# A new order of the attention steps in a fused local and pooled attention with a top-1 mixture of experts

## The chip, the cores and the metric

The kernel runs on one core of a Trainium2 chip. The metric is the device time of one execution in microseconds (us). Five engines work side by side: PE (matmuls; its weight loads are shown apart as PEld), DVE, ACT and POOL (elementwise work), and SP, which here mostly issues transfers. Each runs its own instructions strictly in program order, and they wait for each other through semaphores.

## The reference

Inputs are q, k and v of 8 batches, 8 heads, 576 positions and 64 features, and the weights of a router and of 16 experts.

```python
q_d, k_d, v_d = (x.reshape(B, H, 144, 4, D).mean(axis=3) for x in (q, k, v))
out_up = np.repeat(sm_attn(q_d, k_d, v_d), 4, axis=2)        # attention among means of four
mask = np.abs(pos[:, None] - pos[None, :]) < 4               # local attention, 7 keys wide
out_local = softmax(where(mask, q @ k.T / 8, -1e9)) @ v
x = (out_up + out_local).transpose(0, 2, 1, 3).reshape(4608, 512)
# each token: best of 4 groups, then best of its 4 experts, both by softmax
y = relu(x @ w1[g, e]) @ w2[g, e]                            # 512 -> 1024 -> 512
out = g_w * e_w * y
```

## The kernel before

The attention is cut into 16 units (two batches and two heads each). A unit is a chain of steps, each a method: the transfers `load_k`, `load_q`, `load_v` and `load_windows`; the sums over four positions `pool_q`, `pool_k`, `pool_v`; the local scores `s_local` (72 small matmuls for each head), their shift by the maximum `s_local_out`, `s_local_exp`, `soft_local_sum`, `soft_local`, and the transposes `turn_e`; the pooled scores `s_down`, `s_down_max`, `s_down_exp`, the transposes `turn_pd`, the product `out_down`, its transposes `turn_down`, and `down_store` and `load_down`, which take its result through DRAM into the lower rows of the window tile `vw`; the product `x_bank` of both attentions with `vw`; `store_x`, which writes the tokens to DRAM; `turn_x` and `logits`, the router's scores. A step that copies out of PSUM ends in `_out` and has a letter for its engine (A, D or P: ACT, DVE, POOL). Units 14 and 15 have only one buffer of `x` and of some other tiles (`of`), since the others are given up for the experts' weights (`change`).

After each fourth unit the router works on a quarter of the tokens: `scores_turn`, `choose`, `choose_first` (writes the one-hot tile `oh`), `places` (PE sums of `oh`), `places_out`, `lists_places` (tile `bo`), `lists` (tile `m`, two halves), `lists_add` (PE, tile `tab`). From `tab` come the token lists: `early_list`, `ranks`, `rank_lists`. After three quarters the expert with most room is known (`pick_early`); its first 256 tokens are gathered and computed while attention ends: `turn_in`, eight `hidden` (12 matmuls each) and eight `project` (6 matmuls each), with `weights_in` (transfers) and `weights_split` (each weight split into two parts, on ACT and then POOL or DVE). `begin` and `main` then run the 16 experts, PE almost without a pause.

What sets the order: the text `ORDER` at the end of the file, 966 steps, each with its engine letter where it has a choice. It is read from first to last with automatic scheduling turned off (`tc.manual_schedule()`), so each engine's program is the steps' instructions in the text's order.

```python
for line in ORDER.split("\n"):
    for step in line.split(";"):
        if step.strip():
            name, *args = step.split()
            do(name, [int(a) if a.isdigit() else a for a in args])
```

Of the kernel before, what the change touches and what calls it, by code (L numbers as in the profile page):

```python
# [19 lines left out]
P = 128  # L20
B, H, S, D = 8, 8, 576, 64
# [32 lines left out]
class Attention:  # L54
# [1146 lines left out]
soft_local_sum 0 D; turn_pd 0 2; s_local_out 1 0; load_k 3; turn_pd 0 1; turn_pd_out 0 1 A; turn_pd_out 0 0 A; soft_local 0
turn_pd_out 0 2 A; s_down 1; s_local_exp 1 0; pool_v 0; out_down 0; s_local_exp 1 1; turn_e 0 0; s_down_max 1; clear vs 1
turn_e 0 2; s_down_exp 1 0; soft_down 0 P; s_down_exp 1 1; load_windows 0; turn_e 0 1; soft_local_sum 1 D; turn_e_out 0 2 A
out_down_out 0 D; s_local 2 1; pool_k 2 P; s_local_out 2 1; load_q 3; constants; load_k 4; s_local 2 0; s_down_exp 1 2
turn_e_out 0 0 A; turn_down 0; turn_pd 1 0; turn_pd_out 1 0 A; turn_pd 1 1; load_v 1; s_local_out 2 0; pool_q 3 P; turn_down_out 0
# [4 lines left out]
turn_down 1; turn_pd_out 2 1 A; soft_local_sum 2 D; load_down 0 S; turn_pd_out 2 2 D; pool_v 3; load_v 4; out_down 2  # L1210
turn_down_out 1; s_local_out 3 1; x_bank 0 1; out_down_out 2 A; soft_down 2 D; load_k 5; turn_down 2; x_bank 0 2; x_bank_out 0 1 A
s_down 3; soft_local 2; clear_windows 2; down_store 1 S; pool_q 4 D; turn_down_out 2; x_bank_out 0 2 D; x_bank 0 0; turn_e 2 1
x_bank_out 0 0 A; s_down_max 3; s_down_exp 3 0; turn_x 0 1; turn_e 2 0; load_windows 1; s_down_exp 3 1; turn_x 0 0; turn_x_out 0 1 A
turn_e_out 2 1 D; turn_x_out 0 0 A; s_down_exp 3 2; down_store 2 S; load_down 1 S; turn_e 2 2; turn_e_out 2 0 A; load_k 6
pool_k 4 P; s_local 4 0; s_local_exp 3 1; pool_k 5 D; turn_e_out 2 2 D; store_x 0 A; s_local 4 1; turn_pd 3 0; turn_x 0 2
turn_pd 3 2; turn_pd_out 3 2 A; turn_x_out 0 2 A; s_local_out 4 1; x_bank 1 0; turn_pd_out 3 0 D; s_local_out 4 0; s_local_exp 3 0
x_bank 1 2; x_bank 1 1; load_weights; load_v 5; s_down 4; soft_local_sum 3 P; s_local_exp 4 0; soft_local 3; x_bank_out 1 2 A
turn_pd 3 1; logits 0; x_bank_out 1 0 A; s_down_max 4; s_local_exp 4 1; x_bank_out 1 1 A; turn_pd_out 3 1 A; turn_e 3 0
s_down_exp 4 2; turn_x 1 2; turn_e 3 1; pool_q 5 P; out_down 3; load_windows 2; turn_e_out 3 0 D; soft_local_sum 4 D; load_down 2 S
turn_x 1 0; s_down_exp 4 0; turn_e_out 3 1 A; soft_down 3 P; turn_x_out 1 2 A; s_local 5 0; out_down_out 3 A; load_k 7; load_q 6  # L1220
s_down_exp 4 1; load_v 6; turn_x 1 1; turn_e 3 2; s_local 5 1; turn_e_out 3 2 A; turn_pd 4 0; turn_x_out 1 1 A; turn_x_out 1 0 D
turn_pd_out 4 0 A; turn_down 3; soft_local 4; pool_v 4; s_local_out 5 0; x_bank 2 2; s_local_out 5 1; x_bank_out 2 2 A
turn_down_out 3; logits 1; turn_pd 4 1; load_q 7; x_bank 2 1; s_down 5; s_local_exp 5 1; soft_down 4 P; turn_pd_out 4 1 A
turn_pd 4 2; x_bank 2 0; turn_x 2 2; s_down_max 5; s_down_exp 5 0; s_down_exp 5 1; turn_pd_out 4 2 A; s_down_exp 5 2
x_bank_out 2 1 D; pool_q 6 D; turn_e 4 2; s_local 6 1; turn_x_out 2 2 D; x_bank_out 2 0 D; turn_e_out 4 2 A; pool_k 6 D; s_local 6 0
down_store 3 S; turn_pd 5 2; turn_e 4 0; turn_e 4 1; pool_v 5; turn_e_out 4 0 A; out_down 4; turn_pd_out 5 2 D; s_local_out 6 0
s_local_out 6 1; turn_x 2 0; load_q 8; out_down_out 4 A; load_windows 3; turn_e_out 4 1 D; turn_x_out 2 0 A; turn_down 4
s_local_exp 5 0; load_down 3 S; turn_down_out 4; load_windows 4; s_down 6; s_local_exp 6 0; turn_pd 5 1; turn_x 2 1; s_down_max 6
turn_pd 5 0; turn_pd_out 5 1 A; x_bank 3 0; soft_local_sum 5 D; turn_x_out 2 1 A; x_bank 3 1; turn_pd_out 5 0 A; s_down_exp 6 1
out_down 5; s_down_exp 6 0; down_store 4 S; soft_local 5; out_down_out 5 D; s_local_exp 6 1; turn_e 5 1; x_bank_out 3 0 A; pool_v 6  # L1230
soft_local_sum 6 D; s_local 7 0; soft_down 5 P; s_down_exp 6 2; pool_q 7 P; turn_e_out 5 1 A; x_bank_out 3 1 A; logits 2; load_q 9
x_bank 3 2; turn_x 3 0; turn_down 5; pool_q 8 P; x_bank_out 3 2 A; load_k 8; turn_e 5 0; turn_e 5 2; turn_x_out 3 0 A; pool_k 7 P
turn_down_out 5; turn_x 3 2; load_k 9; s_local_out 7 0; turn_pd 6 1; turn_e_out 5 0 A; pool_k 8 D; turn_e_out 5 2 A; turn_x 3 1
turn_x_out 3 2 A; s_local 7 1; load_down 4 S; turn_x_out 3 1 A; turn_pd_out 6 1 D; turn_pd 6 0; logits 3; store_x 1 A; turn_pd 6 2
load_v 7; turn_pd_out 6 0 A; s_local_out 7 1; s_local_exp 7 1; soft_local 6; turn_pd_out 6 2 D; x_bank 4 0; down_store 5 S
x_bank 4 2; x_bank_out 4 2 D; scores_out 0; load_windows 5; s_down 7; x_bank 4 1; scores_turn 0; x_bank_out 4 1 A; x_bank_out 4 0 D
scores_turn_out 0; out_down 6; turn_e 6 2; store_x 2 A; out_down_out 6 A; turn_e 6 0; s_down_max 7; turn_down 6; soft_down 6 P
pool_v 7; turn_e 6 1; s_down_exp 7 0; s_down_exp 7 2; choose 0; turn_down_out 6; s_local 8 0; s_down_exp 7 1; choose_exp 0
turn_e_out 6 2 D; s_local 8 1; turn_pd 7 0; s_local_out 8 0; turn_e_out 6 0 A; s_local_exp 7 0; turn_x 4 1; turn_e_out 6 1 A
turn_x 4 0; turn_pd 7 2; load_down 5 S; turn_x_out 4 1 A; turn_pd_out 7 0 A; s_local_out 8 1; soft_local_sum 7 D; turn_pd 7 1  # L1240
turn_x 4 2; turn_pd_out 7 1 D; store_x 3 A; turn_x_out 4 2 A; load_q 10; turn_x_out 4 0 A; s_down 8; turn_pd_out 7 2 A; x_bank 5 0
load_v 8; load_k 10; s_local_exp 8 0; choose_first 0; x_bank 5 1; x_bank 5 2; x_bank_out 5 0 A; s_local_exp 8 1; places 0
# [166 lines left out]
```

## Time and profile before

| | |
|---|---|
| runs of the kernel before | 766.26, 775.36, 776.48 us (median 775.36) |
| the profiled execution's own time | 768.92 us |
| its span (first to last instruction) | 767.2 us |
| busy share of the span: PE, DVE, ACT, POOL | 92%, 61%, 47%, 35% |
| mean granted TensorE clock | 0.953 of full |

Times in rows are in us from the span's start; a row of a timeline gives the start, the busy time, the engine, the line, the operation, the tiles written and read and the number of instructions, and in brackets the idle time before it with what ended it ("issue" is a wait for which the profile shows no other engine or transfer). A granted clock of 0.50 is 1.2 GHz and 1.00 is 2.4 GHz.

### The profile page before, as it was taken

To read this page: it belongs to the slowest core of one execution; us is meant where nothing else is said; L and a number is where in the kernel's file an instruction comes from. 1 tells how busy PE (TensorE), PEld (TensorE's weight loads), DVE (VectorE), ACT (ScalarE), POOL (GpSimd) and SP (SyncE) were. 2 spreads that over 40 slices of the span, in tenths; PEclk is the share of its full clock that TensorE was granted. 3 is DMA by queue.
4 is the path that set the end of the run, shared out by engine and by line. 5 is a ranking of instruction groups with operands and counts; after the bars stand their busy time and mean duration, and the time that the engine had idled before them with its cause. 6 is when DMAs were issued, how large, how long until landed. Compare 5 with 4: busy or idle time off the path is not lost. (4 is left out here: it accounts for less than half of the span.)

```text
span 767.2 us, 20003 instructions
## 1 busy us (share of the span) xinstructions
PE 703.1 (92%) x8116; PEld 636.8 (83%) x8117; DVE 464.3 (61%) x840; ACT 359.9 (47%) x791; POOL 268.1 (35%) x313
## 2 busy tenths in 40 slices
PE   6787988898887879999999999999999999999991
PEld 3665766677665769999999999999999999999891
DVE  7776858698885585664545454465465565556510
ACT  1535534575564525553434444445454455556410
POOL 8956547476652652103111221312302312320211
PEclk7879988999999999999999999999999999999997
DMA  8879899989898625855455555555646656665300
GB/s 261 229 201 239 236 247 266 236 232 259 211 207 249 170 88 193 273 171 191 134 177 178 159 176 175 184 184 175 220 149 203 225 165 212 210 213 178 131 26 23
DMA packets 167459, 146.83 MB, mean 191 GB/s; under 512 B 69908, under 2 KB 139540, under 8 KB 167364
## 3 DMA queue, kind: packets, MB, share of 16 engines
q1 hardware_dynamic: 142756, 115.02, 51.4%
q0 software_dynamic: 7088, 21.66, 8.2%
q10 hardware_dynamic: 17520, 8.85, 4.4%
q8 instruction: 64, 1.05, 0.6%
q14 instruction: 31, 0.25, 0.1%
HBM read 124.19 MB, written 22.29 MB: 191 GB/s over the span
## 5 line engine op out<-in xcount | busy, mean ns | idle before, releaser
L866 PE MATMUL ph<-xh,w1h 128*128 128x256 f32 (+13 forms) x512 | 162.3, 318 | 0.0
L837 POOL DMA_INDIRECT xg<-xd,gi x47 | 49.1, 1046 | 320.1 <-ACT yo L940 286.4
L866 PE MATMUL ph<-xl,w1h 128*128 128x256 f32 (+13 forms) x512 | 157.1, 309 | 0.0
L866 PE MATMUL ph<-xh,w1l 128*128 128x256 f32 (+13 forms) x512 | 157.1, 309 | 0.0
L825 DVE TENSOR_TENSOR w2l<-raww,w2h 128x1024 fp32r<-128x1024 f32 x61 | 74.5, 1223 | 72.9 <-ACT w2h L824 70.9
L914 PE MATMUL y<-hl,w2h 128*128 128x416 f32 (+11 forms) x384 | 115.3, 311 | 0.0
L914 PE MATMUL y<-hh,w2l 128*128 128x416 f32 (+11 forms) x384 | 114.3, 308 | 0.0
L824 ACT ACTIVATE w2h<-raww 128x1024 fp32r<-128x1024 f32 x64 | 67.6, 1057 | 73.4 <-PE y L914 61.6
L866 PEld LDWEIGHTS ph<-xh,w1h 128*128 128x128 f32 x512 | 97.4, 191 | 1.5 <-issue 0.2
L866 PEld LDWEIGHTS ph<-xl,w1h 128*128 128x128 f32 x512 | 97.5, 191 | 0.9
L866 PEld LDWEIGHTS ph<-xh,w1l 128*128 128x128 f32 x512 | 97.3, 190 | 0.3
L825 DVE TENSOR_TENSOR w1l<-raww,w1h 128x1024 fp32r<-128x1024 f32 x60 | 73.3, 1223 | 38.8 <-ACT w1h L824 33.8
L871 DVE SCALAR_TENSOR_TENSOR hl<-ph,hh 128x256 fp32r<-128x256 f32 (+13 forms) x128 | 60.3, 475 | 57.3 <-ACT hh L870 57.0
L870 ACT ACTIVATE hh<-ph 128x256 fp32r<-128x256 f32 (+13 forms) x128 | 53.7, 421 | 78.0 <-PE ph L866 75.3
L914 PE MATMUL y<-hh,w2h 128*128 128x416 f32 (+11 forms) x384 | 87.7, 312 | 0.0
L824 ACT ACTIVATE w1h<-raww 128x1024 fp32r<-128x1024 f32 x64 | 67.5, 1056 | 31.8 <-PE ph L866 27.1
L914 PEld LDWEIGHTS y<-hh,w2l 128*128 128x128 f32 x384 | 72.3, 188 | 0.1
L914 PEld LDWEIGHTS y<-hl,w2h 128*128 128x128 f32 x384 | 72.2, 188 | 0.1
L941 POOL DMA_INDIRECT out_dram<-yo,oi x47 | 48.1, 1023 | 67.8 <-ACT yo L940 36.0
L914 PEld LDWEIGHTS y<-hh,w2h 128*128 128x128 f32 x384 | 62.9, 188 | 0.1
L254 PEld LDWEIGHTS b_s<-kt,qT 64*32 64x32 f32 x2304 | 26.9, 116 | 29.2 <-issue 20.0
L427 PE MATMUL b_x<-vw,pt 128*32 128x128 f32 x1152 | 43.6, 298 | 7.5 <-DMA vw<-odd 3.5
(222 smaller groups left out, 1277.0 us busy)
## 6 DMA issues: line engine op xcount, KB each, us to landing
raww<-in_moe_w_dram SPq DMA_DIRECT2D x128, 512.0 KB
vw<-in_v_dram SPq DMA_DIRECT2D x62, 216.0 KB
kt<-in_k_dram SPq DMA_DIRECT2D x16, 576.0 KB
qT<-in_q_dram SPq DMA_DIRECT2D x16, 576.0 KB
xd<-x ACTq DMA_DIRECT2D x15, 576.0 KB
vs<-in_v_dram SPq DMA_DIRECT2D x32, 224.0 KB
vw<-odd SPq DMA_DIRECT2D x16, 144.0 KB
vs<-in_v_dram SPq DMA_DIRECT2D x32, 64.0 KB
```

Of the source, the lines that this page charges most:

```text
L254: nc.tensor.matmul(pt[32 * j : 32 * j + 32, g], s["qT"][r, b, 32 * blk : 32 * blk + 32], self.kt[u % 3][r, b, 32 * blk : 32 * blk + W], st ...
L427: self.nc.tensor.matmul(pt[32 * j : 32 * j + 32, t], self.of("pt", u)[:, 32 * lin : 32 * lin + 32], self.windows(u)[:, lin], start=True, s ...
L824: self.nc.scalar.activation(hi, raw, AF.Copy)
L825: eng.tensor_tensor(out=lo, in0=raw, in1=hi.bitcast(F32), op=ALU.subtract)
L837: self.nc.gpsimd.indirect_dma_start(out=xg[:w], out_offset=None, in_=self.xd[0:rows], in_offset=bass.IndirectOffsetOnAxis(ap=st["gi"][:w, ...
L866: nc.tensor.matmul(ph, a[:, k, cs], st[b][:, k], start=(n == 0), stop=(n == 11))
L870: nc.scalar.activation(hh, ph, AF.Relu)
L871: nc.vector.scalar_tensor_tensor(out=hl, in0=ph, scalar=0.0, in1=hh.bitcast(F32), op0=ALU.max, op1=ALU.subtract)
L914: nc.tensor.matmul(y, a[:, f % 2, cs], b, start=(f == 0 and n == 0), stop=(f == 7 and n == 2))
L941: i = nc.gpsimd.indirect_dma_start(out=self.out, out_offset=bass.IndirectOffsetOnAxis(ap=oi, axis=0), in_=yo[:m], in_offset=None, bounds_c ...
```

## The change

Only `ORDER` is replaced, by another order of the same 966 steps. `load_v` and `load_windows` now make a unit's entry where it is missing (`self.unit(u)` in place of `self.st[u]`), since `load_v 0` may come ahead of other steps of its unit; this adds no instruction. Every buffer, count, shape and function is as before, except for the letters:

| step | before | now |
|---|---|---|
| `pool_k` | 7 on DVE, 9 on POOL | 4 on DVE, 12 on POOL |
| `pool_q` | 7 on DVE, 9 on POOL | 6 on DVE, 10 on POOL |
| `turn_pd_out` | 8 on DVE, 40 on ACT | 14 on DVE, 34 on ACT |
| `turn_e_out` | 13 on DVE, 35 on ACT | 10 on DVE, 38 on ACT |
| `turn_x_out` | 8 on DVE, 40 on ACT | 11 on DVE, 37 on ACT |
| second half of `lists 3`; last `weights_split` | POOL; DVE | DVE; POOL |

Two pieces of the table, the first steps and those of the last quarter's router:

```diff
-shared_rows; clear kt 0; clear kt 1; warm_up 12; masks; masks_out D; load_k 1; clear E 1; s_local 0 1; clear_windows 0; pool_q 0 D
+masks; clear kt 0; clear E 0; masks_out D; load_k 1; warm_up 12; clear vs 0; shared_rows; pool_q 0 D; pool_k 0 D; load_v 0
...
-hidden 2; project 1; places 3; places_out 3; project 2; weights_split 2 w1 P; lists_places 3; lists 3 P; count 3
-weights_split 2 w2 P; hidden 3; lists_add 3; early_list 0; hidden 4; gather_late; project 3; ranks; weights_split 3 w1 P; hidden 5
+choose_first 3; weight 3; weights_split 1 w2 P; project 0; hidden 2; places 3; places_out 3; weights_in 3; lists_places 3
+weights_split 2 w1 P; project 1; hidden 3; lists 3 D; weights_split 2 w2 P; count 3; project 2; hidden 4; lists_add 3; early_list 0
```

**The start.** DVE before: the copies of `shared` into two tiles `pt`, the casts of the mask, then the pooled sums of unit 0 (`qd`, `kd`) and the shift of its local scores.

```order
L162 COPY pt_118<-shared 32x1152
L162 COPY pt_119<-shared 32x1152
L162 CAST idb<-idf 128x128
L162 CAST mask<-edge 128x342
L162 CAST mask<-edge 32x38 x4
L219 TENSOR_REDUCE qd_280<-qT_95 128x288
L234 TENSOR_REDUCE kd_282<-kt_91 128x288
```

DVE now:

```order
L162 CAST idb<-idf 128x128
L162 CAST mask<-edge 128x342
L162 CAST mask<-edge 32x38 x4
L162 COPY pt_118<-shared 32x1152
L162 COPY pt_119<-shared 32x1152
L219 TENSOR_REDUCE qd_240<-qT_95 128x288
L234 TENSOR_REDUCE kd_242<-kt_91 128x288
```

POOL before, at the same place (`edge` is what the mask is cast from, `vw_98` the first window tile):

```order
L123 MEMSET edge 128x38
L127 AFFINE_SELECT edge<-edge 32x38 x8
L129 AFFINE_SELECT edge<-edge 128x38 x2
L112 MEMSET E_130 128x9x10 x2
L140 MEMSET vw_98 128x4608
```

POOL now:

```order
L127 AFFINE_SELECT edge<-edge 32x38 x8
L129 AFFINE_SELECT edge<-edge 128x38 x2
L117 MEMSET kt_91 128x2x3 x2
L112 MEMSET E_129 128x9x10 x2
L114 MEMSET vs_109 48x512
L152 MEMSET shared 32x32
L154 AFFINE_SELECT shared<-shared 32x32 x2
L117 MEMSET kt_92 128x2x3 x2
L112 MEMSET E_130 128x9x10 x2
L140 MEMSET vw_98 128x4608
```

On DVE the two copies moved behind the casts, and on POOL the making of `shared` and the clears of `E_129` and `vs_109` moved ahead of the large clear of `vw_98`.

**The second quarter's choice.** DVE before, around `oh` (L583), on which PE's `places 1` waits; L285 to L287 are `soft_local_sum 11`, L323 to L325 `s_down_max 12`.

```order
L285 TENSOR_REDUCE sl_2924<-E_130 128x18
L286 TENSOR_SCALAR sl_2924<-sl_2924 128x18
L287 RECIPROCAL sl_2924<-sl_2924 128x18
L323 TENSOR_REDUCE mg_112<-b_d_12_3243 128x2
L323 TENSOR_REDUCE mg_112<-b_d_12_3244 128x2
L324 TENSOR_REDUCE mg_112<-b_d_12_3245 128x1
L325 TENSOR_SCALAR mg_112<-mg_112 128x5
L580 TENSOR_REDUCE m2x<-t 128x45
L581 TENSOR_TENSOR o<-t,m2x 128x180
L583 TENSOR_TENSOR oh<-o 128x144
```

DVE now:

```order
L291 TENSOR_TENSOR E_130<-E_130,sl_2923 128x9x76
L162 COPY xT<-b_xt_8_3212 128x3x128
L580 TENSOR_REDUCE m2x<-t 128x45
L581 TENSOR_TENSOR o<-t,m2x 128x180
L583 TENSOR_TENSOR oh<-o 128x144
L323 TENSOR_REDUCE mg_112<-b_d_12_3257 128x2
L323 TENSOR_REDUCE mg_112<-b_d_12_3258 128x2
L324 TENSOR_REDUCE mg_112<-b_d_12_3259 128x1
L325 TENSOR_SCALAR mg_112<-mg_112 128x5
```

`oh` is now written ahead of `s_down_max 12`, and `soft_local_sum 11` stands further up.

**The last quarter's lists.** DVE before, from `bo` to the table's readers (`hl` is the second part of a `hidden`'s result, so each `hl` row stands for one `hidden` on PE):

```order
L662 TENSOR_TENSOR bo<-b,place 128x1152
L657 TENSOR_TENSOR m_4748<-oh,chl 128x9x64
L623 COPY base<-pos_4709 128x16
L871 SCALAR_TENSOR_TENSOR hl<-ph,hh 128x256
L740 COPY th<-tab_4773 128x64
```

DVE now:

```order
L662 TENSOR_TENSOR bo<-b,place 128x1152
L871 SCALAR_TENSOR_TENSOR hl<-ph,hh 128x256
L657 TENSOR_TENSOR m_4767<-oh,chl 128x9x64 x2
L623 COPY base<-pos_4707 128x16
L871 SCALAR_TENSOR_TENSOR hl<-ph,hh 128x256
L740 COPY th<-tab_4798 128x64
```

Both halves of `m` are DVE's now, and two `hidden` instead of one stand between `places 3` and the table.

## Rows read from the trace of the kernel before

**Rows 1.** The page, its first two parts: busy us with share of the span and instructions, and the granted clock and DMA share in 40 slices of the span, in tenths.

```profile
PE 703.1 (92%) x8116; PEld 636.8 (83%) x8117; DVE 464.3 (61%) x840; ACT 359.9 (47%) x791; POOL 268.1 (35%) x313
...
PEclk7879988999999999999999999999999999999997
DMA  8879899989898625855455555555646656665300
```

**Rows 2.** Stretches of the span with each engine's busy time, the granted clock, the DMA share and GB/s: the attention's steady part, its end, the first expert's work beside the last router steps, and the experts.

```profile
20.00:230.00 210.00, 179.03 (x4319) 138.88 (x4307) 162.84 (x375) 110.96 (x373) 132.41 (x168) 0.90 0.91 233
230.00:256.00 26.00, 19.31 (x264) 14.58 (x261) 14.00 (x38) 12.01 (x27) 8.78 (x5) 0.92 0.85 227
256.00:289.00 33.00, 28.54 (x189) 24.80 (x188) 24.09 (x63) 10.39 (x22) 18.36 (x10) 0.91 0.43 127
289.00:767.00 478.00, 462.71 (x3168) 451.30 (x3166) 247.59 (x346) 223.12 (x362) 90.67 (x89) 0.99 0.53 173
```

**Rows 3.** Three of the rows of what PE waited for from 0 to 320 us: total us, times, the longest.

```profile
PE b_s L254 <- issue: 15.4, 8, 3.7
PE b_x L427 <- DMA vw<-odd: 3.5, 1, 3.5
PE tab L670 <- DVE m L657: 2.8, 2, 2.6
```

**Rows 4.** PE's timeline, waits put down to "issue" that are longer than 1 us: the first, the longest and the last of nine.

```profile
31.82 0.70 PE L254 MATMUL b_s<-kt,qT 64*32 64x38 f32 x56 [2.29 <-issue]
...
102.25 0.72 PE L254 MATMUL b_s<-kt,qT 64*32 64x38 f32 x29 [3.69 <-issue]
...
210.61 0.85 PE L254 MATMUL b_s<-kt,qT 64*32 64x38 f32 x44 [1.25 <-issue]
```

**Rows 5.** The stretch between the fifth and the sixth of these waits: busy time of PE, PEld, DVE, ACT and POOL with their instructions in brackets, clock, DMA share, GB/s.

```profile
102.25:124.02 21.77, 21.04 (x506) 16.48 (x507) 15.91 (x40) 10.60 (x38) 12.14 (x15) 0.86 1.06 264
```

**Rows 6.** The page's DMA queues, the one that carries instructions: packets, MB, share of 16 engines.

```profile
q8 instruction: 64, 1.05, 0.6%
```

**Rows 7.** The start: DVE's instructions of line 162 in one stretch (busy us and count, clock, DMA), then timeline rows of DVE, POOL and PE.

```profile
6.12:10.38 4.26, 4.24 (x1) 0.89 0.98 358
...
2.19 1.60 DVE L162 COPY pt<-shared 32x1152 f32<-32x1152 f32 x2 [0.98 <-POOL shared L154]
5.52 5.49 DVE L162 CAST mask<-edge 128x342 bf16<-128x342 f32 x5 [1.49 <-POOL edge L127]
6.09 3.94 POOL L140 MEMSET vw<- 128x4608 f32 x1
11.06 0.44 PE L249 MATMUL b_s<-mask,idb 128*128 128x342 bf16 x1 [4.71 <-DVE mask L162]
12.31 1.34 DVE L234 TENSOR_REDUCE kd<-kt 128x288 f32<-128x1152 f32 x1
13.57 0.51 DVE L268 TENSOR_REDUCE ml<-b_s 128x9 f32<-128x342 f32 x1
14.58 3.93 POOL L140 MEMSET vw<- 128x4608 f32 x1
17.22 1.34 DVE L219 TENSOR_REDUCE qd<-qT 128x288 f32<-128x1152 f32 x1
```

**Rows 8.** The second quarter's `places`: PE's wait for `oh`, DVE's work ahead of `choose_first` (busy us, count, clock, DMA), and the granted clock behind the wait.

```profile
181.61 0.22 PE L596 MATMUL pos<-oh,tri 128*128 128x144 bf16 x1 [1.73 <-DVE oh L583]
...
175.85:179.32 3.47, 3.37 (x9) 1.00 1.09 222
...
183.60:186.90 3.30, 3.30 (x83) 0.50 0.98 269
```

**Rows 9.** The end of the attention: SP's issue of the last windows and of the last but one `load_down`, PE's `x_bank 14`, and ACT's copies of `x_bank 15`.

```profile
230.12 5.87 SPq L204 DMA_DIRECT2D vw<-in_v_dram  x5
237.27 0.74 SPq L420 DMA_DIRECT2D vw<-odd  x1
240.74 3.38 PE L427 MATMUL b_x<-vw,pt 128*32 128x128 f32 x72 [3.47 <-DMA vw<-odd]
...
253.60 0.87 ACT L160 ACTIVATE x<-b_x 128x384 f32<-128x384 f32 x2 [2.43 <-DMA xd<-x]
```

**Rows 10.** The last `lists_add`: PE's stretch from `places 3` to it and PE's wait, DVE's half of `m` there and in the quarter before, and one `hidden` at each clock (us, PE busy and count, clock, DMA share, GB/s).

```profile
266.39:269.29 2.90, 2.90 (x25) 1.00 0.20 9
...
272.11 1.06 PE L670 MATMUL tab<-m,bo 128*128 128x128 bf16 x9 [2.60 <-DVE m L657]
...
270.34 1.71 DVE L657 TENSOR_TENSOR m<-oh,chl 128x576 bf16<-128x576 bf16 x1
234.09 0.76 DVE L657 TENSOR_TENSOR m<-oh,chl 128x576 bf16<-128x576 bf16 x1
...
272.93:275.64 2.71, 2.71 (x16) 0.50 0.03 6
277.04:278.45 1.41, 1.41 (x13) 1.00 0.46 152
```

**Rows 11.** Behind `lists_add`: PE's wait for the second part of a `hidden`.

```profile
285.81 0.33 PE L853 MATMUL xt<-idf,xg 128*128 128x128 f32 x1 [1.34 <-DVE hl L871]
```

**Rows 12.** Groups from 20 to 256 us: busy us and mean ns of one `pool_k` on DVE, and of the dearest of its three instructions on POOL.

```profile
L234 DVE TENSOR_REDUCE kd<-kt 128x288 f32<-128x1152 f32 x5 | 6.7, 1344 | 0.0
...
L226 POOL TENSOR_TENSOR kd<-kd,kt 128x288 f32<-128x288 f32 x9 | 9.2, 1018 | 0.7
```

More of the change, by code (lines that the diff above doesn't have):

```diff
@@ L1201 @@
[L1201 to L1205, printed above, removed]
@@ L1210 @@
[L1210 to L1213, printed above, removed]
@@ L1214 @@
[L1214 to L1242, printed above, removed]
@@ L1288 @@
-x_bank_out 12 1 A; choose_first 2; x_bank 12 0; choose_exp 2; x_bank 12 2; s_down_max 14; x_bank_out 12 0 A; places 2; turn_x 12 0
-load_down 13 S; turn_x 12 1; soft_local_sum 14 D; x_bank_out 12 2 A; s_down_exp 14 0; pool_v 14; s_down_exp 14 2; s_down_exp 14 1
-count 2; turn_x_out 12 0 A; turn_pd 14 0; turn_pd 14 2; turn_x_out 12 1 A; turn_pd_out 14 0 A; turn_pd_out 14 2 A; pool_k 15 P
-pick_early; turn_pd 14 1; s_down 15; load_v 15; turn_pd_out 14 1 A; turn_x 12 2; store_x 12 A; turn_x_out 12 2 A; load_windows 14
@@ new lines @@
+turn_x 0 0; turn_x_out 0 0 A; x_bank_out 1 1 D; turn_e_out 3 1 A; pool_v 4; load_k 6; down_store 2 S; turn_e 3 0; s_down_max 4
+pool_k 5 D; soft_local_sum 4 D; turn_e_out 3 0 A; pool_q 5 P; out_down 3; pool_k 6 P; turn_e 3 2; s_down_exp 4 0; store_x 0 A
+s_local 5 0; x_bank 1 2; s_down_exp 4 1; out_down_out 3 D; turn_e_out 3 2 D; s_local 5 1; s_down_exp 4 2; turn_x 1 1; load_k 7
+load_windows 2; turn_pd 4 2; logits 0; turn_down 3; x_bank_out 1 2 A; s_local_out 5 0; load_down 2 S; turn_pd_out 4 2 A; turn_pd 4 0
@@ new lines @@
+x_bank_out 9 1 A; x_bank_out 9 0 A; lists_add 0; x_bank 9 2; load_k 13; choose_first 1; turn_e 11 1; turn_down 11; lists_out 0
+load_windows 10; s_local_exp 12 1; x_bank_out 9 2 A; turn_x 9 2; s_down_max 12; s_local_exp 12 0; soft_down 11 D; logits 8
+load_down 10 S; places 1; turn_e_out 11 1 D; choose_exp 1; turn_x 9 1; s_down_exp 12 0; turn_down_out 11; load_k 14
+turn_x_out 9 2 A; s_down_exp 12 1; soft_local_sum 12 D; count 1; s_local 13 1; s_down_exp 12 2; turn_x_out 9 1 A; turn_e 11 2
+pool_v 12; turn_x 9 0; turn_e 11 0; turn_x_out 9 0 A; pool_q 13 P; turn_e_out 11 2 A; down_store 11 S; turn_pd 12 0; soft_local 12
@@ new lines @@
+s_local_exp 14 1; choose 2; turn_e_out 13 0 A; out_down_out 13 A; lists_add 1; choose_first 2; turn_down 13; s_down 14; choose_exp 2
+lists_out 1; turn_down_out 13; places 2; s_local_exp 14 0; s_local_exp 15 1; store_x 11 A; x_bank 12 0; s_down_max 14
+s_local_exp 15 0; s_down_exp 14 2; pool_k 15 P; x_bank 12 1; s_down_exp 14 1; s_down_exp 14 0; x_bank_out 12 0 A; load_windows 13
+s_down 15; turn_pd 14 0; count 2; places_out 2; x_bank_out 12 1 A; turn_pd_out 14 0 A; pick_early; down_store 13 S; turn_pd 14 1
```

168 lines of the change are left out of this document (98 added, 70 removed).

## The prediction, on record before the run

> **What bounds the kernel now.** I read the page, then the stretches, then PE's waits, then the timelines at the waits that the new order can touch. From 289 us on PE is busy 462.7 of 478 us at a clock of 0.99 [rows 2], and no step of the changed text issues an instruction there. So the change can act only on the first 289 us. In 20 to 230 us no engine is full: PE is busy 179.0 of 210, but at a granted clock of 0.90; DVE is busy 162.8, ACT 111.0, POOL 132.4; the DMA share is 0.91 [rows 2]. The reader should see a stage with several limits near each other. PE is the nearest: the clock slices below 9 in [rows 1] lie in its first part, but for the last one.
>
> What makes PE idle comes next. The largest entry is no engine: 15.4 us in 8 waits put down to "issue" at one line [rows 3]. Nine such waits are longer than 1 us, from 1.25 to 3.69 us, 18.6 us together, 2.07 us on average [rows 4]. Between two of them PE and PEld ran 506 + 507 = 1013 recorded instructions [rows 5]. The instruction queue carried 64 packets for the 8116 + 8117 instructions of PE and PEld [rows 1, 6], which is 254 per packet, and 1013 is four times 253. So PE stops where one packet of its program ends and the next has not come. The rest are waits on other engines: 3.5 us on a transfer into `vw`, 2.8 us on `m` [rows 3], 1.73 us on `oh` [rows 8], 4.71 us on the mask at the start [rows 7].
>
> On these waits a page of the Trainium skill says otherwise. Runtime: NRT & Kernel Launch, section Instruction fetch mechanics, says that the fetch of the next block is hidden, since an engine issues more slowly than its instruction memory is filled. The trace disagrees: the idle time at these places is 18.6 us. By the page the term for fetches below would be nothing in either order; by the rows it is the widest part of the range.
>
> **The change part by part.** Nothing is added or removed: the steps are the same, and a step's own instructions cost what they did. The letters move work: three `pool_k` and one `pool_q` go from DVE to POOL. One costs DVE 1.344 us and POOL three instructions of about 1 us [rows 12], so DVE loses 5.4 us and POOL gains about 12 us, over a stretch in which POOL is idle for 77.6 of 210 us [rows 2]. I count nothing for it: neither engine is full there, and POOL's idle time covers it. Without that cover it would cost up to 12 us. Now the places.
>
> First, the start. Before, one cast of a 32x38 piece of the mask took 4.24 us, and it lay beside POOL's clear of a window tile, which ran from 6.09 to 10.03 us; PE began unit 0 at 11.06 us [rows 7]. Now the casts stand ahead of that clear. They start earlier than 5.52, because POOL no longer makes `shared` first (my estimate: 0.7 us); without the stretched cast their 5.49 us shrink to about 1.4, and they end near 6.2 us. POOL has two more small clears ahead of the large one, so I place that later than 6.09, at 6.9 to 10.8 us (an estimate too). The two `pt` copies, 0.80 us each [rows 7], now follow the casts. The second falls into the large clear. The nearest row is the stretched cast, which ended 0.35 us after the clear did; by it the copy ends near 11.3 us. Then come the two pooled sums of 1.34 us each, and `s_local_out 0 1` starts at 14.0 us against 13.57 [rows 7]: +0.4 us. A sum itself is not held up: one took 1.34 us beside the second clear, at 17.22 us, as did the one at 12.31 without any [rows 7]. If the copy gets in before the clear, the shift starts at 10.7 us: -2.9 us. I take +0.4, by the nearest row, and keep both ends.
>
> The skill has a rule for this (SBUF — State Buffer, section Who interferes with whom): a DVE copy, cast or tensor_scalar in a two-port mode and a GpSimd instruction exclude each other for a whole instruction, whichever issues first, while a tensor_reduce never contends. It speaks against the change: what it frees the casts from it puts on a copy. The rows on the cast and on the sums agree.
>
> Second, `places 1`. PE waited 1.73 us for `oh`, and the clock then stood at 0.50 for 3.3 us [rows 8]. In front of `choose_first` DVE spent 3.37 us on `soft_local_sum 11` and `s_down_max 12` [rows 8]; now the second stands behind it and the first well ahead. 3.37 is more than 1.73, so this wait should go. The clock's price I take from one `hidden` at either level: 2.71 against 1.41 us, 1.30 us more [rows 10]. Together -3.0 us. But time saved in mid-stage meets a transfer system at 0.91 [rows 2]; what PE gains it may lose again at a later fetch. I take half, -1.5 us, with ends 0 and -3.0.
>
> Third, the end of the attention. `x_bank 14` waited 3.47 us for `load_down 14`. That transfer stands on SP behind `load_windows 15`, which began at 230.12 us, when `x_bank 13` had freed its tile, and took 5.87 us to issue [rows 9]. `x_bank_out 15` then waited for `store_x 14` to leave the only `x` buffer [rows 9]. Both orders keep this chain: `load_windows 15`, `load_down 14`, `x_bank 14`, `store_x 14`, `x_bank_out 15`. Now SP also has the small store of `weight 2` between the first two. What PE is given to do meanwhile hides in the chain. I count 0.
>
> Fourth, the last `lists_add`. PE had 2.90 us of work from `places 3` to it and then waited 2.60 us for `m` [rows 10]. Now there are two `project` and two `hidden` in between, 5.80 us. `m` was ready 5.66 us after `places 3` (from 266.39 to 270.34 + 1.71) [rows 10]. Now DVE makes both halves, behind one more `hl`: `bo` ends as before, and the halves take 0.76 to 1.71 us each, the two times that half of them took [rows 10]. So `m` is ready 5.9 to 7.9 us after, and PE waits 0.1 to 2.1 us; I take 1.0, between, since POOL still works beside DVE here. Saved: 1.6 us, and the `hidden` that ran at 0.50 behind the wait, 1.30 us: -2.9 us, ends -0.5 and -3.8.
>
> Fifth, what is late next. `ranks` now comes ahead of `hidden 5`'s second part, and `project 5` stands behind only two `project`: it may wait 1 to 2.5 us. Before, the wait of this kind was 1.34 us a little further on [rows 11]. I count 0, ends -1.0 and +1.2.
>
> Sum: +0.4 - 1.5 + 0 - 2.9 + 0 = -4.0 us on the profiled execution's 768.92 us (span 767.2), which makes 764.9. That execution is not the middle: the four known are 766.26, 768.92, 775.36 and 776.48, mean 771.8, which is 2.8 above it and 3.6 below the median of the three runs. The forecast for a median is 771.8 - 4.0 = **768 us**.
>
> Then the fetches. I counted PE's instructions between every two packet ends in both orders, and weighed each kind with its start-to-start time at full clock. Before, six of the stretches in the attention hold less than 3.7 us of PE work, the shortest 2.7; now five, the shortest 2.6. So I expect about nine such waits again. Their number is what I know least: it hangs on what each fetch queues behind. One costs 2.07 us [rows 4], and up to 1.30 more where the clock falls.
>
> **The rivals.** *Nothing is gained.* For: the two waits that should shrink are 4.3 of the 42.1 us in which PE idles from 20 to 289 us [rows 2], and the chain at the end of the attention starts only when `x_bank 13` is done; if DVE or the transfers set the pace up to there, PE only waits elsewhere. Against: the fourth place lies behind the chain, and there the DMA share is 0.43 [rows 2]. Time: 772 us.
>
> *Slower, by fetches.* Several loads now stand closer together, and two stretches of PE work below 3 us lie in about the first 70 us of the attention instead of one near its end. From two more waits on, 2 x 3.37 = 6.7 us, the 4.0 us are lost. Four more give 768 + 13.5 = 781 us. For: PE waits at about one packet end in four, so a different deal is likely. Against: the counts of short stretches are six and five.
>
> *Faster by over 2%.* The copy slips in ahead of the clear (-3.3 against my term), the whole of the second place (-1.5), and three fetch waits fewer (-10.1): 768 - 14.9 = 753 us. For: PE's idle time leaves room. Against: all must come together.
>
> **How the numbers follow.** Forecast 0.53 (762 to 773 us), nothing gained 0.27, slower by fetches 0.12, faster by much 0.08. The range from 757 to 779 us takes in the forecast, the case of no gain, the runs' own spread around both (766 to 776 before), and one to three fetch waits either way. A measurement of this kernel can tell about 2% from no change: below 756 or above 787 us around 771.8. Of the last case a half is beyond it, 0.04; of the slower case a third, 0.04; within 2% it is 0.92.
>
> **What would show it.** Right: mask casts below 2 us together and a `pt` copy near 4 us; no wait of `places 1` for `oh`; the wait on `m` at the last `lists_add` below 2 us; `x_bank 14` again waiting for `vw` about 10 us behind `x_bank 13`; eight to eleven "issue" waits over 1 us; the experts as long as before, 478 us from where PE stands at 289 us. Wrong: an attention that reaches `hidden 0` more than 8 us earlier or later than 255.8 us, a first expert that PE runs with more than 4 us of waits, or "issue" waits that sum to less than 10 or more than 28 us.

## The result and the profile after

| | before | changed |
|---|---|---|
| median of 20 runs each, side by side | 773.69 us | 778.67 us |
| lowest to highest | 766.26 to 779.68 us | 772.57 to 784.62 us |
| ratio, 95% interval | | 1.0057 [1.0029, 1.0085] |
| the profiled execution | 768.92 us | 783.48 us |

The new order is slower by about half a per cent, 4.4 us; a second set of runs gave 1.0067 [1.0026, 1.0108]. I had forecast 4 us faster. That 778.67 us still lies inside my range of 757 to 779 us is luck: the direction was wrong, and the range was made wide for other reasons. The two profiled executions lie at opposite ends of their ranges and differ by 14.6 us, three times what the medians do. So the traces are read for places and for single durations, and sizes are taken from ratios, or from a stretch on which several traces agree.

The changed kernel's page, the parts that stand in [rows 1]:

```profile
PE 706.2 (90%) x8116; PEld 637.1 (81%) x8117; DVE 468.1 (60%) x842; ACT 358.1 (46%) x785; POOL 276.7 (35%) x325
...
PEclk8998899998879999999999999999999999999996
DMA  9869989899978536574463555646556556665400
```

POOL has 12 instructions more and DVE two more, as the letters say. The table of letters ahead of the prediction is not complete: `store_x 15` also went from SP to ACT, two `soft_down` from DVE to POOL and two `soft_local_sum` from POOL to DVE, and some `x_bank_out` and `out_down_out` changed engines with their counts kept. Stretches of the changed kernel as in [rows 2]: steady attention, its end, the first expert beside the last router steps, the experts.

```profile
20.00:230.00 210.00, 176.84 (x4230) 137.03 (x4230) 154.83 (x359) 106.22 (x353) 138.83 (x179) 0.90 0.91 227
230.00:264.00 34.00, 24.34 (x352) 17.55 (x349) 19.59 (x54) 13.20 (x36) 9.16 (x7) 0.90 0.79 204
264.00:299.00 35.00, 27.60 (x187) 23.35 (x186) 30.10 (x63) 11.08 (x22) 18.73 (x9) 0.94 0.47 136
299.00:781.00 482.00, 465.79 (x3172) 453.01 (x3170) 247.68 (x346) 223.36 (x363) 92.04 (x90) 0.99 0.52 171
```

In the third row DVE is busy 30.10 of 35 us where it was busy 24.09 of 33 [rows 2], with as many instructions, 63: they take longer, and that is the main finding. What PE waited for from 0 to 300 us in the changed kernel:

```profile
PE b_x L427 <- DMA vw<-odd: 7.7, 2, 3.9
PE b_s L254 <- issue: 6.9, 4, 2.4
PE b_d L300 <- DVE kd L234: 5.8, 1, 5.8
PE b_e L348 <- ACT xT L160: 5.3, 1, 5.3
PE tab L670 <- DVE m L657: 3.7, 1, 3.7
...
PE b_x L427 <- ACT xT L160: 2.6, 2, 2.3
PE b_pd L360 <- ACT PdT L160: 2.1, 1, 2.1
PE xt L853 <- DVE over L1081: 1.9, 1, 1.9
```

Against [rows 3], "issue" at this line fell from 15.4 us to 6.9. In its place stand waits for ACT (5.3, 2.3 and 2.1 us the longest), and the wait for `m` at the last `lists_add`, which I expected to shrink, grew from 2.6 to 3.7 us.

At that wait, PE's first matmul behind `places 3`, DVE's `bo` and `m`, and the matmuls that waited, and last the kernel before's `bo`:

```profile
272.97 0.47 PE L912 MATMUL y<-w2h,hh 128*128 128x512 f32 x1
280.65 1.36 DVE L662 TENSOR_TENSOR bo<-b,place 128x1152 bf16<-128x1152 f32 x1
282.26 1.41 DVE L657 TENSOR_TENSOR m<-oh,chl 128x576 bf16<-128x576 bf16 x2
283.73 0.66 PE L670 MATMUL tab<-m,bo 128*128 128x128 bf16 x9 [3.69 <-DVE m L657]
...
269.06 1.36 DVE L662 TENSOR_TENSOR bo<-b,place 128x1152 bf16<-128x1152 f32 x1
```

So `bo` was done 9.0 us after `places 3` (before: 4.0, from 266.39 to 269.06 + 1.36) and `m` 10.7 us after it (before: 5.7 [rows 10]).

How far one trace can be trusted is shown by the others. PE's "issue" waits over 1 us between 20 and 250 us sum to 9.9 to 18.6 us in nine traces with the old attention (the kernel before and eight of the experiments), 14.3 on average, and to 3.4 to 11.6 us in five with the new one and its stores on ACT, 8.8 on average. PE's waits over 1 us for ACT are 1.0 to 7.3 us, on average 4.4, and 5.4 to 10.9, on average 8.9. The trace of the kernel before is the highest of its nine in the first and the lowest in the second, so the two traces compared here show about twice the usual difference.

**What ACT does meanwhile.** Its timeline in the changed kernel, around the longest of these waits:

```profile
204.18 0.49 ACT L160 ACTIVATE x<-b_x 128x384 f32<-128x384 f32 x1 [0.16 <-PE b_x L427]
210.24 0.38 ACTq L437 DMA_DIRECT2D xd<-x  x1
210.67 0.87 ACT L160 ACTIVATE xT<-b_xt 128x384 f32<-128x384 f32 x2 [6.00 <-DMA vs<-in_v_dram]
```

From 204.67 to 210.24 us ACT stood at the transfer of `store_x 10`, and the row behind it names what ended that: a load of `vs`, with which `store_x` shares no data. The compiled program tells why. SP and ACT raise eight semaphores for their transfers, dealt in turn, and a transfer first waits until the one with the same semaphore, eight transfers back, has landed. `store_x 10` (ACT) and a piece of `load_v 14` (SP) have the same one (`DMAHW1_49`):

```
183 L192 DMA vs_111<-in_v_dram 32x2x256 [waits DMAHW1_49]
257 L437 DMA xd<-x_121 128x9x128 [waits DMAHW1_49]
```

Between the end of ACT's last copy and its issue, `store_x 6` to `10` cost it 2.6, 1.9, 2.9, 3.1 and 5.6 us in the changed kernel. The trace bears this out: all transfers of SP and ACT raise eight semaphores in turn, and each of the five stores was issued 0.02 to 0.07 us after the last landing on its own. For `store_x 6`, `9` and `10` that was a load issued by SP (`vs`, `kt`, `vs`); for `7` and `8` it was the store before. Before, four of its stores cost 1.2 to 2.6 us, 7.8 in all. No view lists this as work; it shows only as idle time in front of ACT's next instruction.

### The profile page after: what moved, and what is told of

Its sections match the earlier page's. It is cut to its first block, busy times and chain, and to the rows that moved or that the text cites. A ratio compares the mean times of both kernels' runs of the same rounds, so it can differ in the third digit from the quotient of the medians.

```text
span 781.8 us, 20021 instructions
## 1 busy us (share of the span) xinstructions
PE 706.2 (90%) x8116; PEld 637.1 (81%) x8117; DVE 468.1 (60%) x842; ACT 358.1 (46%) x785; POOL 276.7 (35%) x325
## 5 line engine op out<-in xcount | busy, mean ns | idle before, releaser
L427 PE MATMUL b_x<-vw,pt 128*32 128x128 f32 x1152 | 42.6, 298 | 10.9 <-DMA vw<-odd 7.7
L846 ACT ACTIVATE xh<-xt 128x256 fp32r<-128x256 f32 (+14 forms) x68 | 27.2, 419 | 43.1 <-PE xt L853 43.1
```

Source lines behind the costliest of these rows:

```text
L427: self.nc.tensor.matmul(pt[32 * j : 32 * j + 32, t], self.of("pt", u)[:, 32 * lin : 32 * lin + 32], self.windows(u)[:, lin], start=True, s ...
L846: self.nc.scalar.activation(hi, x, AF.Copy)
```

## The experiments

Four sets of four kernels; each set ran side by side on one chip with its own runs of the kernel before, and each ratio is against those. Hybrids take the first steps of one order and the remaining steps in the other's sequence. A ratio and the medians of the same runs can differ by some tenths of a per cent; where it matters, both are given.

### Where the loss lies

`h_attention`: the first 838 steps from the new order, the rest from the old (at the top against the kernel before, below against the changed one).

```diff
-shared_rows; clear kt 0; clear kt 1; warm_up 12; masks; masks_out D; load_k 1
+masks; clear kt 0; clear E 0; masks_out D; load_k 1; warm_up 12; clear vs 0
...
 turn_pd 15 1; down_store 14 S; x_bank_out 13 1 A; store_x 13 A
-turn_pd 15 0; lists_places 2; turn_pd_out 15 1 A
+turn_x 12 2; turn_x_out 12 2 A; weight 2; pool_v 15
```

> The new order up to store_x 13 (838 steps: the whole attention up to unit 13), then the remaining steps in the old order. Theory A: in the attention the new order loses about what it gains (fetch waits over 1 us fell from 18.6 to 8.6 us, but PE now waits 10.9 us in four places for ACT, which stands at a store of tokens), and the loss of 5 us lies behind it, at the gather and in the first expert: 0 to +2 us against the kernel before. Rival B: the loss arises in the attention, where the profile of the changed kernel is 5 to 7 us behind at 230 us: +4 to +6 us.

Ratio 0.9976 [0.9944, 1.0007] (medians 767.97 and 768.95 us): 1.8 us faster, if anything. The loss is not in the attention.

`h_expert` and `h_expert_b` are one kernel in two sets: the first 922 steps from the old order, the rest from the new (against the kernel before).

```diff
 turn_x_out 15 1 D; turn_x_out 15 0 A; hidden 0
-weights_split 1 w2 P; weights_in 3; logits 15; scores_out 3; hidden 1; scores_turn 3; project 0
+logits 15; scores_out 3; scores_turn 3; scores_turn_out 3; choose 3; hidden 1; choose_exp 3
```

> The old order up to turn_x_out 15 (922 steps, up to hidden 0), then the new order of the first expert and the last quarter's router. Theory A: the new order of the last section alone costs +3 to +5 us against the kernel before, since the chain to lists_add 3 on DVE lies beside POOL's weight splits and PE waits 2.5 to 4 us for m with two hidden more behind it. Rival B: the section is only late because the gather is late in the changed kernel; alone it costs 0, or gains the 2.9 us that I predicted.

> The old order up to hidden 0 and the new one behind it, once more, beside the next two on one chip: +6 us against before if the first measurement (1.0083) holds on another chip; +2 or less if most of it belonged to that chip.

Ratios 1.0083 [1.0047, 1.0119] and 1.0054 [1.0020, 1.0088]: 4 to 6 us slower, the whole loss or more. With -0.24% for the attention, the +0.83% of the same set makes 0.59%, against the measured 0.57%; little is left for the handover between them, though each of these figures is known to about 0.35% only. From the first `hidden` to the first matmul of the other experts (`phr`), before and in `h_expert`, the stretch takes:

```profile
255.79:289.69 33.90, 29.44 (x192) 25.57 (x191) 24.39 (x63) 10.55 (x23) 18.78 (x10) 0.91 0.44 128
```

```profile
255.56:293.63 38.07, 30.53 (x192) 26.25 (x191) 30.20 (x63) 10.73 (x23) 20.56 (x11) 0.87 0.45 126
```

The same 192 matmuls take 4.2 us longer and the 63 DVE instructions are busy 5.8 us longer. Of the 4.2 us, 1.2 are the longer wait for `m` (3.8 for 2.6), 1.0 the wait for `over` in place of one for `hl` (2.3 for 1.3), 0.9 a new wait for `hl`, and 1.1 PE's own work, more of it at half clock. POOL and DVE in `h_expert`, on the way from `oh` to `m`:

```profile
262.40 2.40 POOL L825 TENSOR_TENSOR w2l<-raww,w2h 128x1024 fp32r<-128x1024 f32 x1 [3.94 <-ACT w2h L824]
264.97 2.40 POOL L825 TENSOR_TENSOR w1l<-raww,w1h 128x1024 fp32r<-128x1024 f32 x1 [0.17 <-ACT w1h L824]
268.64 2.40 POOL L825 TENSOR_TENSOR w2l<-raww,w2h 128x1024 fp32r<-128x1024 f32 x1 [1.26 <-ACT w2h L824]
```

```profile
262.49 0.33 DVE L639 TENSOR_REDUCE sums<-ex 128x45 f32<-128x180 f32 x1
262.85 2.01 DVE L640 TENSOR_TENSOR tw<-sums,o 128x36 f32<-128x36 f32 x1
264.90 0.19 DVE L642 TENSOR_REDUCE two<-tw 128x9 f32<-128x36 f32 x1
265.12 2.28 DVE L643 TENSOR_SCALAR two<-two 128x9 f32<-128x9 f32 x1
268.83 2.28 DVE L612 TENSOR_TENSOR ge<-pos,steps 128x45 f32<-128x45 f32 x1
271.14 0.20 DVE L613 TENSOR_TENSOR c<-ge 128x36 f32<-128x36 f32 x1
```

Each weight part on POOL lasts 2.40 us, and each caught one small DVE instruction, which ended 0.03 to 0.07 us after POOL did: 2.01 us (ended 264.86, POOL 264.80), 2.28 (267.40, 267.37), 2.28 (271.11, 271.04). The first and the second took 0.20 and 0.17 us in the kernel before, where POOL was idle at that moment; the third took 1.00 there, from 267.26, and ended 0.05 us after a POOL part. The kernel before's three instructions and that part:

```profile
264.64 0.20 DVE L640 TENSOR_TENSOR tw<-sums,o 128x36 f32<-128x36 f32 x1
265.10 0.17 DVE L643 TENSOR_SCALAR two<-two 128x9 f32<-128x9 f32 x1
267.26 1.00 DVE L612 TENSOR_TENSOR ge<-pos,steps 128x45 f32<-128x45 f32 x1
...
265.82 2.39 POOL L825 TENSOR_TENSOR w1l<-raww,w1h 128x1024 fp32r<-128x1024 f32 x1 [3.28 <-ACT w1h L824]
```

In `h_expert` the reduce at 262.49 ran in 0.33 us beside POOL, undisturbed. So the chain from `oh` to `m` became about 5 us longer by no work of its own.

The prediction quoted a part of the rule behind this for the start. The same section (the Trainium skill, SBUF — State Buffer, Who interferes with whom) says that a DVE instruction with two SBUF inputs contends with a GpSimd instruction that reads SBUF, that a DVE instruction in a two-port mode, which a tensor_scalar can enter, contends with GpSimd for a whole instruction, and that a reduce never does. All these rows agree with it.

### Are POOL's weight parts the cause?

`x_splits_d` and `x_all_d`: `h_expert` with three and with four letters changed (the last line in the second only).

```diff
-weights_split 1 w2 P
+weights_split 1 w2 D
-weights_split 2 w1 P
+weights_split 2 w1 D
-weights_split 2 w2 P
+weights_split 2 w2 D
-weights_split 3 w2 P
+weights_split 3 w2 D
```

> The kernel with the old order up to hidden 0 and the new one behind it (6 us slower than before), with the letter of three steps changed: weights_split 1 w2, 2 w1 and 2 w2 make their low part on DVE instead of POOL. Theory A: while POOL makes such a part (2.40 us), the next DVE instruction on two SBUF tiles stands until POOL is done (2.01, 2.28 and 2.28 us for instructions that take about 0.2), so the chain to lists_add 3 is 6 us longer than its work; on DVE a part costs 1.21 us. PE's wait for m falls from 3.8 us to 1 to 2.5, and the time to +2 to +4 against before. Rival C: the order of hidden, project and ranks is at fault: the time stays at +6.

> The same with four letters: 1 w2, 2 w1, 2 w2 and 3 w2 on DVE, so that POOL makes only 3 w1 there. Theory A (POOL's parts hold DVE): PE's wait for m falls from 3.8 us to 1 to 2.5, that for over from 2.3 to below 1, and the time is 4 to 7 us below h_expert_b. Rival C (the order of hidden, project and ranks): the time is within 2 us of h_expert_b.

Ratios 1.0004 [0.9957, 1.0050] and 1.0008 [0.9980, 1.0036]; `h_expert_b`, beside the second, stood at 1.0054. So four letters take back 3.5 us, a little less than the 4 to 7 that I expected, and three letters come out below the +2 to +4 us expected of them. The ratios do not tell three from four; the traces below do. In `x_all_d` the stretch from the first `hidden` to `phr`, and DVE on the same way:

```profile
254.44:286.99 32.55, 28.09 (x192) 24.00 (x191) 26.90 (x67) 10.65 (x23) 9.35 (x6) 0.95 0.50 140
...
262.19 0.17 DVE L643 TENSOR_SCALAR two<-two 128x9 f32<-128x9 f32 x1
262.79 1.22 DVE L825 TENSOR_TENSOR w2l<-raww,w2h 128x1024 fp32r<-128x1024 f32 x1
264.93 0.21 DVE L612 TENSOR_TENSOR ge<-pos,steps 128x45 f32<-128x45 f32 x1
```

DVE makes a part in 1.22 us, half of POOL's time, and has four instructions more, yet is busy 3.3 us less. The stretch is 5.5 us shorter than in `h_expert` (38.07 to 32.55), and PE has no wait for `m` left (its longest is now 2.9 us, for `hl`). Here `m` is done 7.1 us after `places 3`, where the kernels with POOL's parts need 10.7 to 10.8. Rival C, the order of `hidden` and `project`, is refuted as the main cause.

`x_last_d` changes only the last of the four letters, and was run in two sets.

> The same kernel (old order up to hidden 0, new behind it) with one letter: the last weights_split, 3 w2, on DVE as in the old order. Theory A: it stops holding the DVE instructions of rank_lists (2.56 us where one takes 0.40); PE's wait of 2.3 us for over and the half clock behind it (3.4 us) shrink: 1 to 3 us less than that kernel, +3 to +5 against before. Rival C: that wait comes from project 5 and rank_lists standing where they do; DVE then does 1.2 us itself, and the time stays at +6.

> The same with the last weights_split, 3 w2, on DVE, once more: theory A, 1 to 3 us below h_expert_b; if the low value of the first measurement (0.9965) holds, 8 us below it, and then this one letter is most of the loss.

Ratios 0.9965 [0.9926, 1.0004] and 1.0043 [1.0009, 1.0077]. Beside `h_expert_b` (1.0054) the ratios show no clear effect of this letter. The low first value had no `h_expert` beside it and did not come again, and the medians of its runs, 773.81 and 773.22 us for the kernel before, do not show it.

The traces settle what the ratios leave open. The first `hidden` lasts 1.7 to 2.9 us from one execution to the next, at a clock of 1.00 or 0.50, so this is the stretch from its end to `phr`, in the kernel before, `h_expert`, `x_last_d`, `x_splits_d` and `x_all_d`:

```profile
258.70:289.69 30.99, 26.53 (x179) 22.88 (x179) 23.62 (x61) 9.90 (x21) 16.41 (x9) 0.94 0.40 114
257.24:293.63 36.39, 28.85 (x178) 24.70 (x179) 29.25 (x61) 9.92 (x21) 19.39 (x11) 0.86 0.42 118
257.38:291.21 33.83, 26.55 (x180) 22.68 (x180) 28.27 (x62) 9.93 (x21) 14.09 (x8) 0.95 0.36 97
259.28:292.70 33.42, 26.65 (x179) 22.57 (x179) 27.18 (x64) 9.81 (x21) 9.13 (x7) 0.94 0.38 117
256.12:286.99 30.87, 26.41 (x178) 22.46 (x179) 25.96 (x65) 9.83 (x21) 8.18 (x6) 0.94 0.50 141
```

The last letter alone takes off 2.6 us, inside theory A's 1 to 3 (33.7 us in its second set; PE's wait for `over` is gone in both), the three others 3.0, all four 5.5. Over all kept traces this stretch lasts 30.8 to 31.0 us with the old order of the section (three traces), 34.8 to 36.4 with the new (seven) and 30.8 to 31.0 with the new and four letters (three). So the letters account for the whole loss in this section, and nothing is left for rival C.

`b_splits_new`: the kernel before, with only the splits at the new places.

```diff
-weights_split 1 w2 P
...
 choose_first 3; weight 3
+weights_split 1 w2 P
...
-weights_split 2 w1 P; lists_places 3; lists 3 P; count 3; weights_split 2 w2 P
+lists_places 3; weights_split 2 w1 P; lists 3 D; weights_split 2 w2 P; count 3
...
-weights_split 3 w1 P; hidden 5; rank_lists
+hidden 5; rank_lists; weights_split 3 w1 P
...
-weights_split 3 w2 D
+weights_split 3 w2 P
```

> The kernel before, with the order of hidden, project, ranks and rank_lists as it is, and only the weight splits at the new order's places and with its letters: 1 w2 behind weight 3, 2 w1 behind lists_places 3, lists 3 on DVE, 2 w2 behind it, 3 w1 behind rank_lists, 3 w2 on POOL. Theory A: the splits beside the chain are most of the loss: +3 to +6 us against before. Rival C: the order of hidden, project and ranks is: -1 to +1.

Ratio 1.0048 [1.0005, 1.0090], 3.7 us slower: inside theory A's range, though not all of it comes from holding DVE: PE waited 5.4 us for `hl` on DVE, but also 3.2 us for a weight part itself, which POOL now made later.

`b_twice`: the kernel before, each of POOL's five parts with c > 0 made twice.

```diff
-        eng.tensor_tensor(out=lo, in0=raw, in1=hi.bitcast(F32), op=ALU.subtract)
+        for _ in range(1 + (eng is self.nc.gpsimd and c > 0)):
+            eng.tensor_tensor(out=lo, in0=raw, in1=hi.bitcast(F32), op=ALU.subtract)
```

> The kernel before with POOL's part of weights_split made twice, the second time over the same values, for the splits 1 w1, 1 w2, 2 w1, 2 w2 and 3 w1 (five more POOL instructions of 2.40 us; POOL is idle for half of that stretch). Theory A: each may hold one more DVE instruction of the chain by about 2 us; PE's wait for m grows from 2.6 us to 5 to 8, and the time by 3 to 7 us. Rival C: POOL's idle time takes them; only lists 3, which stands on POOL behind one of them, comes later: 0 to +1.5 us.

Ratio 1.0119 [1.0085, 1.0153], 9.1 us slower, above the range. What PE waited for there from 252 to 296 us:

```profile
PE y L913 <- DVE hl L872: 5.1, 1, 5.1
PE ph L867 <- POOL w1l L826: 3.5, 1, 3.5
PE pos L596 <- DVE oh L583: 1.3, 1, 1.3
```

Of this, 3.5 us is a wait for POOL's own result, which I had not counted. The 5.1 us is `hl` on DVE, queued behind two held instructions of 2.32 and 2.29 us. So DVE's chain lost about as expected, but PE met the delay at `hl`, ahead of the wait for `m` that I had named.

### ACT at the stores

`a_stores_sp`: the changed kernel with five letters changed; run in two sets, the second beside the changed kernel itself.

```diff
-store_x 6 A
+store_x 6 S
...
-store_x 10 A
+store_x 10 S
```

> The changed kernel with the letter of five steps changed: store_x 6 to 10 are issued by SP instead of ACT. In the changed kernel ACT stands 2.6, 1.9, 2.9, 3.1 and 5.6 us at these five (16.1 us), each waiting until the transfer that had the same semaphore before, eight transfers back in the program, has landed; PE then waits 1.2, 2.3, 2.1 and 5.3 us for ACT. Theory A: those waits of PE go, and the time falls by 3 to 8 us against the changed kernel (+2 to -3 against before). Rival B: the transfers set the pace there (share 0.93), SP stands at the stores instead and the loads come later: no change (+5).

> The changed kernel with store_x 6 to 10 issued by SP, once more. If ACT's standing at the stores costs (theory A): 2 to 4 us below after_again. If the transfers set the pace and PE loses at fetches what it gains from ACT (rival B): within 1 us of it.

> The changed kernel as it is, beside the next three on one chip: +4 to +5 us against before, as measured (1.0057).

Ratios 1.0019 [0.9985, 1.0053] and 1.0000 [0.9966, 1.0034], beside 1.0067 for `after_again`: 5 us gained by five letters, more than expected in the second set. What PE waited for from 20 to 235 us in `a_stores_sp_b`:

```profile
PE b_s L254 <- issue: 8.8, 5, 2.5
PE b_s L254 <- DMA kt<-in_k_dram: 5.0, 2, 3.2
PE b_x L427 <- DMA vw<-odd: 2.7, 1, 2.7
```

The waits for ACT's copies are gone. Rival B is right in part: "issue" and loads of `kt` take 13.8 us now, so some of the gain is given back.

`c_stores`: `h_attention` with the same five letters.

> The new order up to store_x 13, the old one behind it (2 us faster than before by its median), with store_x 6 to 10 issued by SP. If the two gains add (1.8 us for the new attention, about 3 for the stores): -4 to -6 us against before, 0.5 to 0.8%. If the stores only help where the gather is late: -2.

Ratio 0.9948 [0.9910, 0.9985]: 4.0 us faster than before, the lower end of what the sum of the two gains said. The medians, 771.38 and 773.22 us, lie 1.8 us apart, so this run does not prove that the gains add. The kernel before was never run with these five stores on SP, so what they would be worth in the old order is not known.

### The late gather

`a_w2_early`: in the changed kernel the gather on POOL began at 247.62 us, though its list was ready at 239.88; it reads what `weight 2` stores, and that store stood on SP behind `load_windows 15` (6.74 us of issues). One step is moved:

```diff
-load_windows 15; weight 2; lists_out 2
+weight 2; load_windows 15; lists_out 2
```

> The changed kernel with one step moved: weight 2 ahead of load_windows 15, as in the old order, so that its small store of 18 KB stands on SP ahead of 6.7 us of issues. The gather reads what it stores. Theory A: the gather on POOL starts at about 241 us where it started at 247.6, PE no longer waits 3.1 us for xg, and the kernel comes out 2 to 3 us below the changed one (+2 to +3 against before). Rival B: PE only waits longer for x_bank 14 or for the weights, and the time is the changed kernel's (+5).

Ratio 1.0077 [1.0044, 1.0109]: no gain. The gather did start early, at 235.78 us. PE's wait moved:

```profile
243.06 4.07 PE L427 MATMUL b_x<-vw,pt 128*32 128x128 f32 x72 [6.51 <-DMA vw<-odd]
```

`x_bank 14` waited 6.51 us for `load_down 14`, where it had waited 3.79 in the changed kernel, and the 3.14 us for `xg` were gone: rival B.

### Both causes together

`a_all_d` has the four split letters, `a_letters` those and the five store letters; no step of the new order is moved.

> The changed kernel with weights_split 1 w2, 2 w1, 2 w2 and 3 w2 on DVE instead of POOL. Theory A: 3 to 5 us below after_again, as between h_expert_b and x_all_d: 0 to +2 against before. Rival C: within 1 us of after_again.

> The changed kernel with both: store_x 6 to 10 on SP and the four splits on DVE, nine letters in all and no step moved. If the two causes are apart and add: 5 to 8 us below after_again, -1 to -4 us against before. If only one of them is real: +1 to -1 against before.

Ratios beside `after_again` (1.0067): 1.0030 [0.9993, 1.0067] with the splits alone, 1.0000 with the stores alone, 0.9954 [0.9921, 0.9988] with both. The splits give 0.37%, the stores 0.67%, together 1.04%; measured 1.13%. Each ratio is known to about 0.35%, so the splits' part is clear by the stretch above (31.0 us in `a_all_d`) rather than by this ratio. Within that the two causes add, and they are more than the whole loss: with nine letters the new order is 3.5 us faster than the kernel before, which has its own stores on ACT. Its first-expert stretch:

```profile
253.77:286.21 32.44, 28.06 (x191) 23.96 (x191) 26.74 (x67) 11.01 (x23) 9.53 (x7) 0.95 0.50 151
```

## Why the prediction failed, point by point

- **The start: right in size and mechanism, in another copy.** The mask casts took 1.70 us together. It was the first `pt` copy that was stretched beside the large clear, not the second: it took 4.96 us of the two copies' 6.05, since the clear began at 5.97 us, where I had put 6.9. `s_local_out 0 1` began at 14.26 us, where I had 14.0 and before had 13.57 [rows 7].
- **`places 1`: right about the wait, not about the gain.** PE no longer waited for `oh`. But within 10 us of it, on either side, it waited 2.3 and 2.1 us for ACT, which stood at its stores.
- **The end of the attention: right.** `x_bank 14` waited 3.79 us, before 3.47 [rows 9]. The store of `weight 2`, counted 0, did make the gather late, and `a_w2_early` gained nothing by moving it, because `x_bank 14` waits then anyway.
- **The last `lists_add`: the step that failed.** I wrote "`bo` ends as before" and so "`m` is ready 5.9 to 7.9 us after, and PE waits 0.1 to 2.1 us". But `bo` ended 9.0 us after `places 3` in place of 4.0, `m` was ready after 10.7, and PE waited 3.7 us. The saving of 2.9 us became a loss: the section behind the first `hidden`, -2.9 us in my sum, is 4.7 us longer in the changed kernel's trace (from 266.06 to 301.79 us, 35.73 for 30.99) and 5.4 in `h_expert`. I took the way to `bo` as it lasted before, where POOL was mostly idle at the moments that matter, and added only what DVE itself has more to do. I did not look where the moved `weights_split` steps put POOL's 2.40 us parts. With four of them on DVE, `m` is ready 7.1 us after, inside my 5.9 to 7.9. A part of the rule was in my own text, at the start's term, and [rows 10] showed a half of `m` at 1.71 us beside POOL and 0.76 elsewhere.
- **What is late next: the wait right, the letter beside it not.** I had allowed a wait of 1 to 2.5 us where 1.34 had been; PE waited 1.86 us, though for `over` behind the lists and not for `project 5` (2.3 in `h_expert`, with 3.4 us of half clock behind it). I counted nothing for the last `weights_split` on POOL; that letter alone is worth 2.6 us in the trace of `x_last_d`.
- **The fetches: wrong, and in the other direction.** Nine "issue" waits of 18.6 us became five over 1 us, 8.6 us together. I had expected nine, and below 10 us I had called wrong. The rival "slower, by fetches" is refuted. That PE stops at the ends of packets holds: between two such waits its recorded instructions, semaphore instructions with them, number 512, 512, 768, 1024, 1024, 768, 1280 and 1536 in the kernel before, all multiples of 256. Which ends are late differs between executions, though: with the same steps up to there, `h_expert` has five such waits, and the changed kernel has five in one trace and two in another. So nine was a high draw and not a property of the order. What was gained did not arrive at the end, since PE waited more for ACT at the stores, 10.9 us in this trace. That these two cancel was not in any of my cases: I had costed `store_x` nowhere, as its steps are the same.
- **"Nothing is gained"** came nearest in its argument (PE only waits elsewhere) for the attention, but it ended on no change, and I had looked for the gain, not the loss, behind the attention.
- **The signs.** Two more of my signs of being wrong came up: a first expert with more than 4 us of PE's waits (3.7 for `m`, 1.9 for `over` and 1.2 for `hl` alone), and a `hidden 0` more than 8 us late (264.38 us for 255.79). The second says little, since `hidden 0` began at 251.41 us in another execution of the same kernel.

What stays open: why a given packet end is late in one execution and not in the next, and whether the new order still gains anything over the old one if both have their stores on SP.

## What to carry to other kernels

When a step moves, look up what runs beside it on POOL, and cost each small DVE instruction on a dependent chain at what the neighbour's instruction lasts (here 2.0 to 2.3 us for 0.2), not at its own duration. Work given to an idle POOL is free only where DVE's chain is not being waited for; DVE did the same part in 1.22 us without holding itself up. An engine that computes should not issue a transfer that must first wait for an earlier one, its own or another queue's, to land: five stores moved to SP were worth 5 us here. And read waits from more than one trace before forecasting from them: the "issue" waits of one program summed to 8.6 us in one execution and 3.4 in another.

## What the runs showed of the hardware

- A small DVE tensor_tensor or tensor_scalar that starts inside a POOL weight part ended 0.03 to 0.07 us after it, whatever its own size: 2.01, 2.28 and 2.28 us for 36, 9 and 45 columns. A reduce beside the same parts took 0.33 us.
- The same subtraction of 128x1024 takes 2.40 us on POOL and 1.22 us on DVE.
- I had not expected a load issued by SP to stop ACT: 5.6 us at one store, ended by the landing of `vs`.
- PE's "issue" waits come at multiples of 256 of its instructions (512 to 1536 apart in the kernel before), at some of these places and not at others.
